# A burst of throwaway matmuls and sums on a zeroed buffer ahead of the first stage of a convolution kernel

## The chip, the cores and the metric

The kernel runs on one core of a Trainium2 chip. A core has a matmul engine (TensorE, PE in the profile, with its weight loads as PEld), a vector engine (DVE), a scalar engine (ACT), GpSimd (POOL), and SyncE (SP), which here issues all DMAs. The engines run beside one another, each in its own program order, and wait for one another through semaphores. On-chip data lie in SBUF, 128 partitions wide; matmul results go to PSUM, which has eight banks of 128 partitions by 512 f32 values.

The metric is the device time of one execution in microseconds; smaller is better.

## The reference

A long causal convolution by FFT, then a gated block: a short convolution of five taps that gives a gate, and two projections.

```python
def _attn_ref(x, h):                    # x: 8 x 6400 x 128, h: 6400 x 128
    L = 2 * S
    Xf = np.fft.rfft(x, n=L, axis=1)
    Hf = np.fft.rfft(h, n=L, axis=0)
    Yf = Xf * Hf[None, :, :]
    return np.fft.irfft(Yf, n=L, axis=1)[:, :S, :]

def _moe_ref(x, w_val, conv_w, w_out):
    gate_pre = np.zeros((B, S, D), dtype=np.float32)
    for k in range(K):                  # K = 5
        gate_pre += conv_w[k][None, None, :] * xp[:, k:k + S, :]
    gate = 1.0 / (1.0 + np.exp(-gate_pre))
    val = x @ w_val
    return gate * val @ w_out
```

## The kernel before

The sequence of 6400 is split as 100 x 64, so that the transforms become matmuls in f32 with constant matrices. For each of the eight batches and for the filter h there are four stages: stage 1 (transform over 100, `Forward`), stage 2 (transform over 64 and the product with the filter's spectrum, `Spectrum` for h and `Product` for x), stage 3 (`s3_quads`) and stage 4 (`Chunk.s4`), and behind them the gated block (`Chunk`, `Gates`). All matmuls address the array in parts: quarters of 64 rows by 64 columns of weights (stages 1 and 3), or halves of 128 rows by 64 columns (the rest). The profile names a matmul's tile by rows and columns, 50*64 for example; each matmul has one weight load (LDWEIGHTS) and one MATMUL. Since a helper records every operation (line 98), nearly all instructions carry that one line, and they are told apart by tiles.

The order on each engine is the order of the program's text; nothing is reordered.

What the change and the steps around it touch:

- `dt` (line 123) is one SBUF buffer of 128 x 16384 f32. At the start its first 12,800 columns, as `gh` (line 125), take stage 1 of the filter h. `gl` (line 131) is free at that time; later the weights of the gated block are decoded in it, when the first stage is over (line 508).
- `pair()` (line 203) hands out tiles of two PSUM banks, alternately from two pools of two tiles each.
- `fh` and `fx` (line 493) are stage 1 of the filter and of batch 0. Lines 494 to 496 ask for the first eight tiles of h, 256 KB each, and for the constant matrix r1; the first three go to `x_sb`, the others into m4_sb.
- `sums` (line 223) makes sum and difference of a loaded tile: the subtraction on POOL (line 229), the sum on the engine that it is given, DVE here (line 230), and then asks for the next tile. Lines 498 and 499 call it twice ahead of the loop.
- `half` (line 233) makes 16 matmuls of quarters on one tile's sums (line 241) and returns two copies from PSUM to `gh` or `gy`. The loop of lines 500 to 507 does 32 such halves, 16 for h and 16 for batch 0; the first copy goes to ACT (line 506), the second to ACT and DVE in turn.
- Behind this loop come stage 2 of both, from line 509, and then the loop over the batches, from line 575.

Of the kernel before, what the change touches and what calls it, by code (L numbers as in the profile page):

```python
# [13 lines left out]
ALU = mybir.AluOpType  # L14

S = 6400
C = 128
# [4 lines left out]
HP = 64  # L22
# [88 lines left out]
def longconv_moe(ctx: ExitStack, tc: tile.TileContext, x, h, r1, m2, r3, m4, w64, out):  # L111
    nc = _Engines(tc)
    B = x.shape[0]
    MUL, ADD = ALU.mult, ALU.add
# [8 lines left out]
    dt = cp.tile([128, N2 * 2 * C], F32, name="dt")  # L123
# [7 lines left out]
    gl = cp.tile([128, N2 - LATE, N1], F32, name="gl")  # L131
# [71 lines left out]
    def pair():  # L203
        pairs.append(pairs.pop(0))
        return pairs[-1].tile([128, 2, 512], F32, name="pt2", tag="pt2")
# [288 lines left out]
    fh.load()  # L494
    nc.sync.dma_start(r1_sb, r1)
    fh.load(len(xh) - 1)
    order = [(f, i) for f in (fh, fx) for i in range(NS)]
    for f, _ in order[:2]:
        f.sums(nc.vector)
# [75 lines left out]
    for b in range(B):  # L575
# [8 lines left out]
        for g in range(NS):  # L584
# [9 lines left out]
            if b == 0 and g < NKB:  # L594
                a = CH * g
# [96 lines left out]
```

## Time and profile before

| | |
|---|---|
| median of 2 runs | 1002.66 us (1001.01 to 1004.32) |
| the profiled execution | 1006.82 us |
| its span, first to last instruction | 1005.0 us |
| mean granted PE clock | 0.986 |
| instructions on PE, DVE, ACT, POOL | 21360, 939, 916, 551 |

In the page, "busy" is the time in which an engine works, with its share of the span. The rows of PE's clock have one digit for each fortieth of the span, in tenths of full speed. The chain follows the work that ended last back to its releasers. In the timeline a row has the start and the time taken in us, the engine and operation, the tile written and read, how many were merged, and the idle time before, with what ended it. A row of the groups by form ends with the busy time in us and the mean of one in ns, then the engine's idle time before them. A row of the windows has the stretch, its length, the busy time of PE with the number of its matmuls, the granted clock, the DMAs' share and GB/s. SPq is SyncE's queue, which issues DMAs.

### The profile page before, as it was taken

The page shows a single profiled execution, that of the slowest core. Times are in us where ns is not written, and L with a number is a line of the kernel's source. Part 1 is how long each engine was busy: PE and PEld are TensorE (multiplying, and loading weights), DVE is VectorE, ACT ScalarE, POOL GpSimd, SP SyncE. Part 2 cuts the span into 40 slices and gives each one's busy share as a digit, 9 for nine tenths or more (in the row PEclk, how much of TensorE's full clock was granted, in tenths as well). Part 3 has the DMA queues.
Part 4 walks back from the last instruction along what each step waited for, and adds up shares of the span by engine and source line. Part 5 has one row for each costly group of instructions (what it writes and reads, how often), then busy time and mean ns, then how long its engine had stood idle before and what let it go on. Part 6 is the DMA issues. An engine that isn't in the chain of part 4 may idle for free.

```text
span 1005.0 us, 46982 instructions
## 1 busy us (share of the span) xinstructions
PE 940.5 (94%) x21360; PEld 793.5 (79%) x21360; DVE 702.8 (70%) x939; ACT 475.5 (47%) x916; POOL 544.5 (54%) x551
## 2 busy tenths in 40 slices
PE   7897778999999999999999998999989999999987
PEld 7797778787978878887878778887887878786753
DVE  5499217977398747977398756977399755978366
ACT  4521434445543653546444554445544553534465
POOL 6467434785277744785177743784367752760032
PEclk9898999999999999999999999999999999999989
DMA  7783854756467545755467555665467554750012
GB/s 253 244 272 149 283 204 158 225 157 194 134 229 214 156 154 194 230 159 166 150 223 218 153 159 186 216 176 170 145 211 221 151 178 159 229 140 34 31 42 91
DMA packets 96838, 177.33 MB, mean 176 GB/s; under 512 B 43392, under 2 KB 49792, under 8 KB 96640
## 3 DMA queue, kind: packets, MB, share of 16 engines
q1 hardware_dynamic: 96640, 174.34, 55.6%
q8 instruction: 167, 2.74, 1.1%
q14 instruction: 31, 0.25, 0.1%
HBM read 141.55 MB, written 32.77 MB: 173 GB/s over the span
## 4 chain that ended last, share of the span: by engine, by line
PE 90%; issue 5%; DVE 3%; POOL 1%; ACT 1%; DMA 0%; POOLq 0%; DVEq 0%; ACTq 0%
PE pt L98 90%; DVE gl L98 1%; DVE dt L98 1%; POOL gl L98 1%; ACT dt L98 1%; DVE gy L98 0%; POOL dt L98 0%; DMA x<-hl 0%; DVE sd L98 0%; DVE m_sb L98 0%; POOLq L688 0%; ACT gl L98 0%; ACT yl L98 0%; ACT gy L98 0%; DVEq L98 0%
## 5 line engine op out<-in xcount | busy, mean ns | idle before, releaser
L98 PE MATMUL pt<-r_sb,gy 64*64 64x128 f32 (+1 forms) x8192 | 267.3, 273 | 20.3 <-issue 11.5
L98 PEld LDWEIGHTS pt<-r_sb,gy 64*64 64x64 f32 (+1 forms) x8192 | 235.8, 130 | 63.8 <-ACT gl L98 20.4
L98 POOL TENSOR_TENSOR sd<-x 128x256 f32<-128x256 f32 x236 | 197.4, 860 | 154.2 <-issue 124.2
L98 POOL TENSOR_TENSOR gy<-gy,h 128x512 f32<-128x512 f32 (+1 forms) x182 | 221.6, 1241 | 63.6 <-DVE h L98 27.7
L98 ACT COPY dt<-pt 128x512 f32<-128x512 f32 (+3 forms) x269 | 155.2, 581 | 193.9 <-PE pt L98 191.6
L98 PEld LDWEIGHTS pt<-m_sb,dt 128*64 128x64 f32 x4096 | 191.5, 137 | 35.3 <-issue 22.7
L98 PEld LDWEIGHTS pt<-gy,m 128*64 128x64 f32 x3008 | 179.1, 135 | 43.8 <-issue 23.6
L98 PE MATMUL pt<-gy,m 128*64 128x128 f32 x3008 | 193.3, 278 | 17.5 <-issue 12.0
L98 PE MATMUL pt<-m_sb,dt 128*64 128x100 f32 x4096 | 198.0, 250 | 2.9 <-DVE dt L98 2.4
L98 DVE COPY dt<-pt 128x512 f32<-128x512 f32 (+1 forms) x136 | 92.5, 680 | 132.1 <-PE pt L98 125.6
L98 PE MATMUL pt<-r_sb,sd 50*64 50x100 f32 x4608 | 143.2, 258 | 17.2 <-issue 11.2
L98 DVE TENSOR_TENSOR gy<-pt,h 128x1024 f32<-128x1024 f32 (+1 forms) x99 | 116.8, 1180 | 46.3 <-PE pt L98 46.3
L98 DVE SCALAR_TENSOR_TENSOR gl<-yl,w_sb,gl 128x500 f32<-128x500 f32 x147 | 130.6, 892 | 24.6 <-ACT gl L98 22.1
L98 PEld LDWEIGHTS pt<-r_sb,sd 50*64 50x64 f32 x4608 | 128.9, 142 | 22.2 <-issue 14.5
L98 DVE SCALAR_TENSOR_TENSOR dt<-pt,w_sb,dt 128x500 f32<-128x500 f32 (+7 forms) x216 | 132.9, 631 | 13.5 <-POOL dt L98 3.8
L98 ACT COPY gy<-pt 128x400 f32<-128x400 f32 x248 | 110.2, 496 | 41.2 <-PE pt L98 32.8
L98 ACT ACTIVATE dt<-pt,w_sb 128x500 f32<-128x500 f32 (+1 forms) x64 | 40.0, 625 | 170.2 <-PE pt L98 169.4
L98 PE MATMUL pt<-dt,w_sb 128*64 128x500 f32 (+2 forms) x480 | 116.0, 561 | 0.8 <-DVE dt L98 0.4
L98 POOL TENSOR_TENSOR dt<-dt,p 128x500 f32<-128x500 f32 (+1 forms) x64 | 66.4, 1038 | 82.5 <-DVE dt L98 58.0
L98 DVE TENSOR_TENSOR h<-pt,h 128x1024 f32<-128x1024 f32 (+1 forms) x91 | 107.3, 1179 | 2.3
L98 ACT COPY yl<-pt 128x500 f32<-128x500 f32 (+1 forms) x96 | 54.5, 568 | 83.9 <-PE pt L98 83.9
L98 DVE TENSOR_TENSOR gl<-pt,gl 128x500 f32<-128x500 f32 (+1 forms) x48 | 31.7, 661 | 54.5 <-PE pt L98 50.8
(40 smaller groups left out, 568.5 us busy)
## 6 DMA issues: line engine op xcount, KB each, us to landing
m<-m SPq DMA_DIRECT2D x90, 512.0 KB, 4.7
h<-hd SPq DMA_DIRECT2D x84, 512.0 KB, 3.9
x<-xl SPq DMA_DIRECT2D x118, 256.0 KB, 3.4
out<-dt SPq DMA_DIRECT2D x56, 250.0 KB, 5.8
out<-yl SPq DMA_DIRECT2D x40, 250.0 KB, 2.5
m_sb<-m SPq DMA_DIRECT2D x13, 375.0 KB, 4.5
hd<-h SPq DMA_DIRECT2D x8, 512.0 KB, 5.1
m_sb<-m SPq DMA_DIRECT2D x6, 512.0 KB, 6.5
```

Source lines behind the costliest of these rows:

```text
L98: return self._tc.keep_in_program_order(call(*args, **kwargs))
```

## The change

Between the first loads (line 496) and the first sums (line 497) new code is put. It zeroes the first 12,800 columns of dt, called z: columns 0 to 4095 by DVE, the rest by POOL. Then `throwaway` makes 290 matmuls on z into four PSUM banks (two tiles from `pair`): 70 of 128 x 128 weights by 512 moving columns (`slow`), and between them ten groups of small ones. Five groups have six rounds of four quarters, with 64 or 50 columns of weights that lie packed or at a step of two or four elements, and 64 or 128 moving columns; in one group the output is strided too. One group has 20 matmuls of 64 rows by 128 columns of weights and 64 moving columns. Three groups have 20 matmuls of 128 rows by 64 columns of weights and 128 moving columns, packed or strided, and the last has 20 with 50 moving columns. The last four wide matmuls write the four banks.

Then `throwaway_vector` makes three rounds, each with banks of four and of eight columns: ACT copies half of a PSUM view to gl, DVE adds that to the other half and writes dt, DVE subtracts likewise, and ACT makes a small copy to dt. Two copies of 512 columns on ACT end it. None of what it writes is read by the rest of the kernel: the first stage overwrites dt afterwards. Nothing is removed or moved.

```diff
--- before.py
+++ after.py
@@ -494,6 +494,86 @@
     fh.load()
     nc.sync.dma_start(r1_sb, r1)
     fh.load(len(xh) - 1)
+
+    z = dt[:, :12800]
+    zo = dt
+    nc.vector.memset(z[:, :4096], 0.0)
+    nc.gpsimd.memset(z[:, 4096:], 0.0)
+
+    def throwaway():
+        p = pair()
+        q = pair()
+        banks = [p[:, 0], p[:, 1], q[:, 0], q[:, 1]]
+
+        def mm(rows, cols, n, r0=0, c0=0, rhs=None, lhsT=None, bank=0, o=None):
+            o = banks[bank][c0 : c0 + cols, :n] if o is None else o
+            a = z[r0 : r0 + rows, :cols] if lhsT is None else lhsT[r0 : r0 + rows]
+            b = z[r0 : r0 + rows, 128 : 128 + n] if rhs is None else rhs[r0 : r0 + rows]
+            nc.tensor.matmul(o, lhsT=a, rhs=b, start=True, stop=True)
+
+        def slow(n):
+            for _ in range(n):
+                mm(128, 128, 512, bank=3)
+
+        def quarters(n, cols, width, lhsT=None, blocks=False):
+            for _ in range(n):
+                for r, c in ((0, 0), (1, 0), (1, 1), (0, 1)):
+                    o = None
+                    if blocks:
+                        o = banks[r][c * HP : c * HP + cols].rearrange("p (d b m) -> p d b m", d=4, b=4)[:, 0, ::3]
+                    mm(64, cols, width, r * HP, c * HP, lhsT=lhsT, bank=r, o=o)
+
+        e8 = z[:, 1024:2048].rearrange("p (k t) -> p k t", t=2)
+        e16 = z[:, 2048:4096].rearrange("p (k t) -> p k t", t=4)
+        m2v = z.rearrange("p (d k t) -> p d k t", k=100, t=2)
+        m4w = z.rearrange("p (d k t) -> p d k t", k=100, t=4)
+        slow(12)
+        quarters(6, 64, 64)
+        slow(6)
+        quarters(6, 64, 64, e8[:, :64, 1])
+        slow(6)
+        quarters(6, 50, 64, e8[:, :50, 1], True)
+        slow(6)
+        quarters(6, 64, 128, e8[:, :64, 1])
+        slow(6)
+        quarters(6, 64, 128, e16[:, :64, 1])
+        slow(6)
+        for _ in range(10):
+            for r in range(2):
+                mm(64, 128, 64, r * HP, bank=r)
+        slow(6)
+        for rhs in (None, m2v[:, :, 7], m4w[:, :, 7]):
+            for _ in range(10):
+                for c in range(2):
+                    mm(128, 64, 128, 0, c * HP, rhs=rhs, bank=2)
+            slow(6)
+        for _ in range(10):
+            for c in range(2):
+                mm(128, 64, 50, 0, c * HP, bank=2)
+        for i in range(4):
+            mm(128, 128, 512, bank=i)
+        return p, q
+
+    def throwaway_vector(p, q):
+        def ops(n, d, v, o, eng):
+            eng(o, v)
+
+        zv = zo.rearrange("p (n c d) -> p n c d", c=2, d=C)
+        v4 = p[:, 0].rearrange("p (d b m) -> p b m d", b=4, m=32)
+        v8 = p.rearrange("p r (d b m) -> p b m (r d)", b=4, m=32)
+        v = nc.vector
+        tmp = [gl.rearrange("p n t -> p (n t)")[:, 512 * i : 512 * i + 512].rearrange("p (b m d) -> p b m d", b=2, m=32) for i in range(2)]
+        for i in range(3):
+            for w, d in ((v4, 4), (v8, 8)):
+                t = tmp[i % 2][:, :, :, :d]
+                nc.scalar.copy(t, w[:, 2:])
+                for op, n in ((ADD, zv[:, 1:32]), (ALU.subtract, zv[:, 63:32:-1])):
+                    v.tensor_tensor(out=n[:, :, :, :d].rearrange("p n c d -> p c n d"), in0=w[:, :2, 1:], in1=t[:, :, 1:], op=op)
+                nc.scalar.copy(zv[:, 0, :, d : 2 * d], w[:, 0:2, 0])
+        nc.scalar.copy(zo[:, 0:512], q[:, 0])
+        nc.scalar.copy(zo[:, 0:512], q[:, 1])
+
+    throwaway_vector(*throwaway())
     order = [(f, i) for f in (fh, fx) for i in range(NS)]
     for f, _ in order[:2]:
         f.sums(nc.vector)
```

## The prediction

> **What bounds the kernel now.** I read the page first, for the span, the engines and the chain; then the timeline of the first 10 us, because the change stands ahead of the first stage; then the windows of PE, for the pace and the clock there.
>
> ```profile
> span 1005.0 us, 46982 instructions
> PE 940.5 (94%) x21360; PEld 793.5 (79%) x21360; DVE 702.8 (70%) x939; ACT 475.5 (47%) x916; POOL 544.5 (54%) x551
> PEclk9898999999999999999999999999999999999989
> PE 90%; issue 5%; DVE 3%; POOL 1%; ACT 1%; DMA 0%; POOLq 0%; DVEq 0%; ACTq 0%
> ```
>
> PE is busy 94% of the span and is 90% of the chain that ended last. There is no slack behind it into which whole microseconds of extra PE work at the head could be moved: what delays PE's first real matmul delays the end by as much, unless the first stage is held by something else. The timeline shows what holds it:
>
> ```profile
> 0.73 1.28 ACT L98 ACT_TABLE_LOAD   x1 [0.73 <-PEq L682]
> 0.74 0.39 SPq L98 DMA_DIRECT2D x<-hl  x1
> 2.59 2.33 SPq L98 DMA_DIRECT2D m_sb<-hl  x5
> 3.44 0.42 DVE L98 TENSOR_TENSOR sd<-x 128x256 f32<-128x256 f32 x1 [3.44 <-DMA x<-hl]
> 3.92 13.14 PE L98 MATMUL pt<-r_sb,sd 50*64 50x100 f32 x347 [3.92 <-DVE sd L98]
> 5.28 0.43 DVE L98 TENSOR_TENSOR sd<-x 128x256 f32<-128x256 f32 x1 [1.42 <-DMA x<-hl]
> 6.43 0.43 DVE L98 TENSOR_TENSOR sd<-x 128x256 f32<-128x256 f32 x1 [0.72 <-DMA x<-hl]
> ```
>
> The engines start at about 0.74 us. The first load ends DVE's wait at 3.44 us, its sum releases PE at 3.92 us, and PE then works on without a long wait until 17 us. Only these 3.44 us are free cover at the start; later waits for loads are 1.42 and 0.72 us.
>
> **The change, part by part.** It removes nothing. Everything added is on the zeroed buffer z, which is dt; the first stage's real results go into the same dt (line 251 through the copies), and each engine works in program order. So the sum on DVE (line 230) stands behind all added DVE work, the first copies on ACT (line 506) behind the added ACT copies, and the first real matmul (line 241) behind the added matmuls and behind DVE's sum. The end of the added DVE work takes the place of 3.44 us.
>
> **Loads and POOL: nothing.** Eight tiles of x are asked for ahead of the new code and land under the burst. SP's ninth load waits for the first sums and is shifted with them, as before. The subtraction on POOL (line 229) stands behind POOL's memset of 8,704 columns, and so do the matmuls that read z beyond column 4,096.
>
> ```profile
> L98 POOL TENSOR_TENSOR gy<-gy,h 128x512 f32<-128x512 f32 x168 | 211.9, 1283 | 63.6 <-DVE h L98 27.7 <-issue 15.6 <-PE pt L98 15.2
> L98 DVE TENSOR_TENSOR gy<-pt,h 128x1024 f32<-128x1024 f32 x92 | 112.0, 1217 | 39.4 <-PE pt L98 39.4
> L98 DVE TENSOR_TENSOR gy<-pt,h 128x512 f32<-128x512 f32 x7 | 4.8, 692 | 7.0 <-PE pt L98 7.0
> L98 DVE COPY dt<-pt 128x512 f32<-128x512 f32 x128 | 87.9, 687 | 125.8 <-PE pt L98 125.6
> L98 ACT COPY dt<-pt 128x512 f32<-128x512 f32 x129 | 75.7, 587 | 164.7 <-PE pt L98 162.4 <-ACT gl L98 2.3
> L98 ACT COPY gy<-pt 128x400 f32<-128x400 f32 x248 | 110.2, 496 | 41.2 <-PE pt L98 32.8
> ```
>
> At POOL's 1283 ns for 512 columns the memset takes 22 us at most. The matmuls that need it come after 54 wide ones, so at either price below 23 or 46 us after the burst's start at 5 us: no wait.
>
> **The memset on DVE.** 4,096 columns; no row shows one. DVE's step from 512 to 1024 columns is 525 ns, 1.03 ns a column: 4.2 us. A quarter of that, 1.1 us, is my lower bound. I take the nearest row, 4.2 us. The burst then starts at 0.74 + 4.2 = 5.0 us. The Trainium skill, "VectorE: DVE Perf Modes", section on zero memsets issued as uint32, has a memset at one cycle per element, which would be about 4.3 us; no trace here shows one.
>
> **The burst.** I count 70 matmuls of 128x128 weights by 512 columns (12, six after each of nine groups, 4), and 220 small ones in ten groups: 120 of quarters, 20 of row halves, 80 of column halves. The rows for their pace:
>
> ```profile
> 332.76 0.88 PE L98 MATMUL pt<-r_sb,sd 50*64 50x100 f32 x32
> 333.56 1.06 PE L98 MATMUL pt<-yl,w_sb 128*64 128x500 f32 x4
> 336.35 0.87 PE L98 MATMUL pt<-r_sb,sd 50*64 50x100 f32 x32
> 337.04 1.93 PE L98 MATMUL pt<-r_sb,gy 64*64 64x128 f32 x64
> 338.79 0.87 PE L98 MATMUL pt<-r_sb,sd 50*64 50x100 f32 x32
> 988.55 1.01 PE L98 MATMUL pt<-gl,w_sb 128*64 128x500 f32 x4
> 62.00:82.00 20.00, 20.00 (x351) 1.00 0.81 274
> L98 PE MATMUL pt<-dt,w_sb 128*64 128x500 f32 x416 | 107.0, 585 | 0.8 <-DVE dt L98 0.4 <-DVE gl L98 0.2
> L98 PEld LDWEIGHTS pt<-m_sb,dt 128*64 128x64 f32 x4096 | 191.5, 137 | 35.3 <-issue 22.7 <-DVE dt L98 8.0 <-PE pt L98 2.1
> ```
>
> Two pairs of column halves by 500 columns take 1.01 us from first start to last end, one matmul 0.585, so the second pair starts 0.425 us after the first: 0.85 ns a column for a pair. The 64 quarters from 337.04 to 338.79 us take 27.3 ns each, 109 a quad of 128 columns, again 0.85 ns a column. So f32 costs 0.85 ns a column, whatever the rows, where both column halves are served by matmuls of their own.
>
> The wide matmul has no row: one instruction, one stream of moving columns, 128 columns of weights. Its lower bound is the pair's pace, 512 x 0.85 = 0.43 us. Its upper bound is the two halves served in turn by the one stream, 0.86 us. As instruction it is nearest to one half's matmul, and the pair gets its pace from two instructions that each bring their stream; a single stream that needs 0.85 ns a column for 64 columns of weights should need twice that for 128. I take 0.86 us: 70 x 0.86 = 60.2 us. With 0.43 it is 30.1. Of pages, two bear on it. The Trainium skill, "FP8 and Floating Point Precision", TensorE Precision Notes, lets true FP32 pass the array four times; four passes at its 2.4 GHz would be 0.85 us, 59.7 us for the 70. The Trainium skill, "Perfetto Trace Analysis", Engine Utilization, halves the array's rate for FP32_LOW_HIGH, which would be 0.43 us and 29.9 us; the halves' 0.85 ns a column agrees with the latter, the full width no run shows.
>
> The small ones, at the clock of those rows: 72 quarters with 64 columns between half of 27.3 ns and the 21.6 that 100 columns cost (336.35 to 337.04 over 32), near the latter because the loads of weights are as many: 1.5 us. 48 quarters with 128 columns by 27.3: 1.3 us. Strided weights I put at nothing beyond that, since gy's weights in the 27.3 ns row have the same stride of two elements. 60 column halves with 128 columns by 20.00/351 = 57 ns: 3.4 us, strided moving operands included as that row has them. 20 column halves with 50 columns, half of 57 to 57: 0.8 us. 20 row halves with 64 columns, 27 to 80 ns: 1.0 us. Together 8.0 us.
>
> Switches between tile shapes: 32 matmuls take 0.69 us from 336.35 to the next start, but 0.80 from 332.76 where the shape changes to 128 rows. That is 0.11 us, times 20 switches 2.2 us.
>
> **The clock.**
>
> ```profile
> 8.00:10.00 2.00, 2.00 (x56) 1.00 1.05 403
> 13.00:15.00 2.00, 1.94 (x82) 1.00 0.61 183
> 20.00:21.00 1.00, 1.00 (x32) 0.50 0.51 197
> 97.11 0.70 PE L98 MATMUL pt<-r_sb,gy 64*64 64x128 f32 x8 [5.24 <-DVE gy L98]
> 96.00:106.00 10.00, 8.19 (x252) 0.75 0.42 130
> ```
>
> From 8 to 10 us PE makes 28 matmuls a microsecond, about as at clock 0.50 at 20 us, and 41 at 13 us: the start runs at half clock, whatever the column shows before its first event, some 8 us from 3.92 on. The burst will pay for it instead, 3.4 to 8.3 us at half pace, 1.7 to 4.2 lost: 2.8 us. Will the first stage then find full clock? At 97.11 us PE had idled 5.24 us and the ten microseconds around read 0.75, so it had gone back to half. The tail below idles PE for 9 us. I count no gain; kept full clock would be worth up to 4 us.
>
> **The tail.** DVE's twelve sums have 248 or 496 columns a row: 512 columns cost 692 ns and a column 1.03, so 421 and 676 ns. ACT's copies of 256 and 512 columns: 587 ns, and (587-496)/112 = 0.81 ns a column, 380 and 587. Each round on DVE is two small sums, a hand-over, ACT's 512-column copy (it waits for the buffer that the small sums read), a hand-over, two large sums: 0.84 + 0.05 + 0.59 + 0.05 + 1.35 + 0.05 = 2.93 us. Three rounds and the first copy: 9.2 us, entirely behind the last matmul, since its bank is written last. Reads and writes with strides like these stand in the rows (dt from pt, 687), so nothing more for them. The two last ACT copies (1.2 us) run beside DVE's last sum and the first real matmuls; the small copies, beside DVE.
>
> **The sum.** 5.0 + 60.2 + 8.0 + 2.2 + 2.8 + 0.2 (last matmul's latency) + 9.2 = 87.6 us at the tail's end, against 3.44 us: 84.2 later. Loads that have landed spare the first stage at most the 1.42 and 0.72 us, at half clock about 1. Net +83. The profiled execution took 1006.82 us, so 1090; it stands 4.2 above the median of 1002.66, so against the median 1086. The start-up bounds move this by -3 and +2, the clock by -5 and +2, the small matmuls by 2 either way.
>
> **The rivals.**
> A: the wide matmul runs at the pair's pace, 0.43 us. For it: 0.85 ns a column wherever the trace looks. Against it: nowhere does one stream feed both halves. 1086 - 30 = 1056. This is also where the halved rate of the page leads.
> B: weight loads come out from under the wide matmuls. A load of 64 columns takes 137 ns; 128 columns with no other tile to work beside might show 0.14 to 0.27 us each, 70 times: +10 to +19, 1096 to 1105. For it: in the rows loads always have another half at work. Against it: PEld is busy 79% beside PE's 94% with hardly a gap, so loads are hidden at a far denser rate.
> C, not slower: the burst is covered by the start's own waits. Place: ahead of line 499. The cover is 3.44 us for the first load, 2 for the next loads, 4 of half clock. It decides only if start, burst and tail together stay under about 10 + 20 = 30 us; without start, tail and small matmuls (26 us) the 70 would have to take under 4 us, 0.06 us each, seven times faster than any row's pace. It would read 1003 to 1022.
>
> **How the numbers follow.** My forecast 0.73, A 0.18, B 0.07, C 0.02. The likeliest gives 1086, its own range 1076 to 1094. The range that takes in A and the cheaper half of B is 1050 to 1100, with 0.9 of the chance before the bounds' own error. A change of 2%, 20 us, is about what a measurement of this kernel can tell from none; all cases but C are slower by more: slower 0.97, same 0.02, faster 0.01.
>
> **What would show it.** In the timeline after: DVE's memset ending near 5 us; wide matmuls starting every 0.86 us (A: 0.43; B: over 1.0); the last one ending near 78 us; DVE's sums until 88 us; the first sd<-x then; the first stage again at half clock; from there on the same stages, shifted. If the time differs while the shift is as summed, the later stages have changed, which I hold to be nothing. What would make it wrong above all is the price of one wide matmul: every 0.1 us of it is 7 us.

## The result, and the profile after

The changed kernel takes 1096.67 us (median of 2 runs, 1096.43 to 1096.91) against 1002.66 us before: 1.0926 times the time, 95% interval 1.0872 to 1.098. In a later comparison it took 1099.68 us (4 runs) against 1004.38 us (17 runs), 1.095 times (1.0912 to 1.0987). The forecast was 1086 us with a range of 1050 to 1100.

The page after:

```profile
span 1094.7 us, 48185 instructions
PE 1023.1 (93%) x21940; PEld 836.0 (76%) x21940; DVE 712.7 (65%) x952; ACT 479.6 (44%) x930; POOL 551.4 (50%) x552
PEclk9998799889999999999999999999999999999999
PE 90%; issue 4%; DVE 4%; ACT 1%; POOL 1%; POOLq 0%; DVEq 0%; ACTq 0%
```

PE has 21940 matmul instructions instead of 21360: 580 more, for 290 more matmuls in the text. So each f32 matmul of the text is two weight loads and two MATMUL instructions; the sentence ahead of the prediction that gives it one of each is wrong by that factor. This count is what the prediction misread.

The timeline after, from the start to the first real matmul (start, time taken, engine and operation, count, idle time before):

```profile
0.73 7.35 POOL L98 MEMSET dt<- 128x8704 f32 x1 [0.29 <-POOLq L762]
1.66 3.47 DVE L98 MEMSET dt<- 128x4096 f32 x1 [1.66 <-PEq L762]
5.18 80.62 PE L98 MATMUL pt<-dt 128*128 128x512 f32 x580 [5.18 <-DVE dt L98]
7.05 0.34 PEld L98 LDWEIGHTS pt<-dt 128*128 128x128 f32 x1 [0.52 <-issue]
7.91 0.34 PEld L98 LDWEIGHTS pt<-dt 128*128 128x128 f32 x1 [0.52 <-issue]
9.24 0.19 PEld L98 LDWEIGHTS pt<-dt 128*128 128x128 f32 x1 [0.24 <-issue]
9.67 0.19 PEld L98 LDWEIGHTS pt<-dt 128*128 128x128 f32 x1 [0.24 <-issue]
86.02 0.74 DVE L98 TENSOR_TENSOR dt<-pt,gl 128x248 f32<-128x248 f32 x2 [80.89 <-PE pt L98]
86.85 0.17 ACT L98 COPY dt<-pt 128x8 f32<-128x8 f32 x1 [2.35 <-DVE dt L98]
86.91 0.59 ACT L98 COPY gl<-pt 128x512 f32<-128x512 f32 x1
87.53 1.26 DVE L98 TENSOR_TENSOR dt<-pt,gl 128x496 f32<-128x496 f32 x2 [0.78 <-ACT gl L98]
88.82 0.17 ACT L98 COPY dt<-pt 128x16 f32<-128x16 f32 x1 [1.32 <-DVE dt L98]
88.89 0.38 ACT L98 COPY gl<-pt 128x256 f32<-128x256 f32 x1
89.30 0.74 DVE L98 TENSOR_TENSOR dt<-pt,gl 128x248 f32<-128x248 f32 x2 [0.51 <-ACT gl L98]
95.27 1.09 DVE L98 TENSOR_TENSOR sd<-x 128x256 f32<-128x256 f32 x3
95.74 7.67 PE L98 MATMUL pt<-r_sb,sd 50*64 50x100 f32 x224 [9.94 <-DVE sd L98]
```

The burst runs from 5.18 to 85.8 us. A wide matmul shows two weight loads, 0.43 us from one to the next at full clock and 0.86 at half clock, up to about 8.9 us. The half clock there is read from this spacing: the trace's first record of the clock is the change to full at 8.85 us. The tail takes 86.02 to 95.27 us, and DVE's first real sum starts at 95.27 us instead of 3.44: 91.8 us later. The small groups, in windows from each group's first matmul to the next wide one (stretch, length, PE busy and matmuls; edges count once more):

```profile
17.48:18.34 0.86, 0.86 (x49) 1.00 0.00 0
23.69:24.57 0.88, 0.88 (x50) 1.00 0.00 0
29.92:30.74 0.82, 0.82 (x50) 1.00 0.00 0
36.09:37.56 1.47, 1.47 (x49) 1.00 0.00 0
42.91:44.56 1.65, 1.65 (x49) 1.00 0.00 0
49.91:52.29 2.38, 2.38 (x42) 1.00 0.03 7
57.63:59.96 2.33, 2.33 (x41) 1.00 0.00 0
65.31:67.76 2.45, 2.45 (x41) 1.00 0.00 0
73.12:75.45 2.33, 2.33 (x41) 1.00 0.00 0
80.80:82.10 1.30, 1.30 (x41) 1.00 0.00 0
24.57:29.92 5.35, 5.35 (x19) 1.00 0.00 0
```

The ten groups take 16.5 us. The last row is one stretch of six wide matmuls: 5.35 us where 12 instructions of 0.429 make 5.15. The 0.2 that is left falls at the two changes of tile shape, about 0.1 us each; ten times over it is 2.0 us.

What became of the 91.8 us later on shows in one and the same DVE instruction, the first of a pair of TENSOR_SCALAR behind the first stage, before (first fence) and after (second):

```profile
53.63 1.68 DVE L98 TENSOR_SCALAR gl<-gl 128x261 int32<-128x261 int32 x2
```

```profile
146.87 1.68 DVE L98 TENSOR_SCALAR gl<-gl 128x261 int32<-128x261 int32 x2
```

There the shift is 93.2 us; at the end the spans differ by 1094.7 - 1005.0 = 89.7 us. So the head accounts for it; what moves by three microseconds either way behind it is no larger than what executions of one and the same program differ by (999.97 to 1010.44 us for the kernel before in one comparison), and is not explained here.

### The profile page after: what moved, and what is told of

The parts are those of the page before. It is cut to its first block, busy times and chain, and to the rows that moved or that the text cites. A ratio compares the mean times of both kernels' runs of the same rounds, so it can differ in the third digit from the quotient of the medians.

```text
span 1094.7 us, 48185 instructions
## 1 busy us (share of the span) xinstructions
PE 1023.1 (93%) x21940; PEld 836.0 (76%) x21940; DVE 712.7 (65%) x952; ACT 479.6 (44%) x930; POOL 551.4 (50%) x552
## 4 chain that ended last, share of the span: by engine, by line
PE 90%; issue 4%; DVE 4%; ACT 1%; POOL 1%; POOLq 0%; DVEq 0%; ACTq 0%
PE pt L98 90%; DVE dt L98 2%; DVE gl L98 1%; ACT dt L98 1%; POOL gl L98 1%; DVE sd L98 0%; DVE gy L98 0%; POOL dt L98 0%; ACT gl L98 0%; DVE m_sb L98 0%; POOLq L768 0%; ACT yl L98 0%; DVEq L98 0%; POOLq L98 0%; ACTq L98 0%
## 5 line engine op out<-in xcount | busy, mean ns | idle before, releaser
L98 PE MATMUL pt<-r_sb,gy 64*64 64x128 f32 (+1 forms) x8192 | 270.6, 275 | 15.7 <-issue 6.7
L98 PEld LDWEIGHTS pt<-r_sb,gy 64*50 64x50 f32 (+1 forms) x8192 | 238.7, 131 | 59.5 <-ACT gl L98 21.2
L98 POOL TENSOR_TENSOR gy<-gy,h 128x512 f32<-128x512 f32 (+1 forms) x182 | 221.7, 1240 | 64.1 <-DVE h L98 32.5
L98 ACT COPY dt<-pt 128x512 f32<-128x512 f32 (+5 forms) x277 | 157.0, 571 | 194.5 <-PE pt L98 183.0
L98 PE MATMUL pt<-gy,m 128*64 128x128 f32 x3008 | 193.0, 278 | 17.5 <-issue 12.0
L98 PE MATMUL pt<-dt 128*128 128x512 f32 (+6 forms) x580 | 80.6, 342 | 5.2 <-DVE dt L98 5.2
```

The costliest lines, as they stand in the source:

```text
L98: return self._tc.keep_in_program_order(call(*args, **kwargs))
```

## The experiments

Two theories stood against each other after the result. **P, passes:** every f32 matmul of the text is two PE instructions, each at 0.85 ns a column, whatever the width of its weights. **S, streams** (the prediction's): one instruction costs 0.85 ns a column for 64 columns of weights, and 128 columns fed by one stream cost twice that.

**Wide matmuls as two halves.**

```diff
-                mm(128, 128, 512, bank=3)
+                for c in range(2):
+                    mm(128, 64, 512, 0, c * HP, bank=3)
...
-            mm(128, 128, 512, bank=i)
+            for c in range(2):
+                mm(128, 64, 512, 0, c * HP, bank=i)
```

> Each of the 70 wide matmuls (128x128 weights, 512 columns) becomes two of 128x64 by 512 columns; the rest of the change stays. Theory P (passes): the trace after holds two PE instructions for every matmul of the text, 580 for 290, and each takes 0.429 us for 512 columns; a pair of halves is then four instructions that run two by two, 0.86 us a pair, as one wide matmul. Time as after the change, about 1097 us, within 3 us, less up to 2 us for shape switches that fall away. Theory S (the prediction's: one stream feeds the two halves in turn, two streams at once feed them side by side): a pair takes 0.43 us, 30 us less, about 1067 us.

1093.28 us, 1.0875 times the time before (1.0836 to 1.0913). The groups by form of the first 84 us and the window of one stretch of six such pairs:

```profile
L98 PE MATMUL pt<-dt 128*64 128x512 f32 x280 | 64.1, 609 | 5.2 <-DVE dt L98 5.2
```

```profile
24.49:29.79 5.30, 5.30 (x30) 1.00 0.00 0
```

140 matmuls of the text are 280 instructions, and six pairs take 5.30 us where six wide ones took 5.35. The halves do run two by two: one after the other, 280 instructions of 0.429 us would take 120 us, and PE is busy for 64.1 us with them. Side-by-side halves gain nothing over a full-width matmul: S is wrong, P holds.

**Wide matmuls in bf16.** They read the same zeros as bf16, so that this part is another computation.

```diff
+        zb = z[:, :320].bitcast(mybir.dt.bfloat16)
+        def wide(bank):
+            nc.tensor.matmul(banks[bank], lhsT=zb[:, :128], rhs=zb[:, 128:], start=True, stop=True)
...
-                mm(128, 128, 512, bank=3)
+                wide(3)
```

> The 70 wide matmuls read the same zeros as bf16 (128x128 weights, 512 columns); small groups and tail stay f32. Theory P: a bf16 matmul is one PE instruction and the profile shows 510 instead of 580 on the zeroed buffer; at the pace of 0.429 us for each it would be 30 us less, about 1067 us, and if each of the two f32 instructions also runs at half pace, 0.21 us for one bf16, 45 us less, about 1052 us. Theory S says nothing of bf16.

1048.81 us, 1.0426 times (1.039 to 1.0461): some 48 to 51 us less than the changed kernel, by its two medians. Windows of two stretches of bf16 matmuls (five of the six of each are in the records, and the windows start at the first of these), and DVE's first real sum in the timeline:

```profile
10.84:12.01 1.17, 1.17 (x5) 1.00 0.00 0
13.12:14.29 1.17, 1.17 (x5) 1.00 0.07 14
```

```profile
49.36 1.09 DVE L98 TENSOR_TENSOR sd<-x 128x256 f32<-128x256 f32 x3
```

The first sum comes at 49.36 instead of 95.27 us, 45.9 earlier, which is 70 x (0.858 - 0.216) = 44.9 and about 0.1 us less around each of the ten groups. The other 2 to 5 us of the time lie behind the head and are not explained. The median distance of two such matmuls is 0.216 us and each is one instruction, 62 of the 70 being in the records. So an f32 matmul costs four times a bf16 one, as two instructions at half pace. The Trainium skill, "FP8 and Floating Point Precision", TensorE Precision Notes, has four passes for true FP32: the cost agrees, 0.858 against 0.216 us, though the trace shows two instructions.

**Without the small groups.** The 220 small matmuls are left out and the 70 wide ones stand in one row.

```diff
-        quarters(6, 64, 64)
-        slow(6)
...
+        slow(54)
```

> The ten groups of small matmuls are left out, the 70 wide ones, the memsets and the tail stay. By the trace after: the groups take 16.5 us from their first start to the next wide one, and the shape switches add 0.2 us to each of ten wide groups: 18.5 us less, about 1078 us. By the prediction's prices (8.0 us and 2.2 us) 10 us less, about 1086 us.

1075.67 us, 1.0705 times (1.0671 to 1.0738), 21 to 24 us less than the changed kernel. DVE's first real sum in the timeline:

```profile
77.78 1.08 DVE L98 TENSOR_TENSOR sd<-x 128x256 f32<-128x256 f32 x3
```

It comes 95.27 - 77.78 = 17.5 us earlier; a microsecond of the 18.5 is missing because full clock came at 10.8 us here, against 8.9. What the time shows beyond that lies behind the head, where executions differ by as much, and is not explained. The prediction's 10.2 us for groups and switches are refuted.

**Without the tail.** The kernel that ran had kept the small groups, so its time stands against the changed kernel, and only the differences of the expectation apply, not its absolute times.

```diff
-    throwaway_vector(*throwaway())
+    throwaway()
```

> As the run without small groups, and the whole tail of ACT copies and DVE sums is left out too, so that nothing reads the burst's results. Against that run: if the tail lies wholly on the path, its 9.4 us go (from the last matmul's end at 85.8 us to DVE's first real sum at 95.3 us in the trace after). If the clock is then kept full, because PE no longer idles for 10 us, half of the 5.3 us that the first stage ran at half clock goes as well: 12 us in all, about 1066 us; if the loads or the sums bind the first stage instead of the clock, 9.4 us alone, about 1069 us. A rival that has part of the tail covered by the loads: less than 7 us.

1087.27 us, 1.0812 times (1.078 to 1.0843), 9.4 to 12.4 us less. The timeline and a window of ten microseconds of its first stage (busy time of PE, PEld, DVE, ACT, POOL with counts, then the granted clock):

```profile
85.51 2.29 PE L98 MATMUL pt<-r_sb,sd 50*64 50x100 f32 x96
90.72 1.78 PE L98 MATMUL pt<-r_sb,sd 50*64 50x100 f32 x64 [0.47 <-DVE sd L98]
92.98 1.61 PE L98 MATMUL pt<-r_sb,sd 50*64 50x100 f32 x55 [0.47 <-DVE sd L98]
137.36 1.68 DVE L98 TENSOR_SCALAR gl<-gl 128x261 int32<-128x261 int32 x2
```

```profile
85.00:95.00 10.00, 7.98 (x281) 6.43 (x280) 7.90 (x11) 5.33 (x12) 6.02 (x8) 1.00 0.46 129
```

PE's first real matmul comes at 85.51 instead of 95.74 us, 10.2 earlier: all of the tail is on the path. The clock stays full, but PE now waits for DVE's sums: 64 instructions, two halves of the first stage, take 92.98 - 90.72 = 2.26 us, of which PE works 1.78. The time, 9.4 to 12.4 us less, does not tell whether a gain of clock came on top of the tail.

**Without small groups and tail**, the comparison that the last expectation describes.

> The run without the tail had still held the small groups; here both are left out, so that it stands against the run without small groups (1075.7 us). By the difference that the tail made in the full burst (PE's first real matmul at 85.5 instead of 95.7 us): 10 us less, about 1066 us, with full clock at the first stage worth nothing more, because DVE needs 1.13 us for each half of the first stage there and PE's 0.73 us at full clock do not come to bear. If full clock counts, 12 us or more less, 1064 us or under. First real matmul near 67 us: 5.2 + 2.0 for cold clock + 70 x 0.858.

1066.45 us, 1.0633 times (1.0579 to 1.0688), with a wide spread of 1061 to 1072. That is 9.2 us under the run without small groups by the medians, 7 by the ratios. The timeline:

```profile
67.82 2.29 PE L98 MATMUL pt<-r_sb,sd 50*64 50x100 f32 x96
116.14 1.68 DVE L98 TENSOR_SCALAR gl<-gl 128x261 int32<-128x261 int32 x2
```

The first real matmul comes at 67.82 us; by 5.18 + 2.4 (full clock at 9.95 us) + 70 x 0.858 it should come at 67.6. The tail costs its own length. A gain from kept clock does not show: from the first real matmul to the first TENSOR_SCALAR behind the first stage this run takes 116.14 - 67.82 = 48.3 us, and the other trace without a tail 137.36 - 85.51 = 51.9. All twelve traces of this case, with tail, without it and before, lie from 48.3 to 51.9 us, so a gain of some 2 us or less could hide in this spread.

**A small burst alone, as a warm-up, on the kernel before.**

```diff
+    nc.gpsimd.memset(dt[:, :640], 0.0)
+    p = pair()
+    for n in (512, 256):
+        nc.tensor.matmul(p[:, 0, :n], lhsT=dt[:, :128], rhs=dt[:, 128 : 128 + n], start=True, stop=True)
```

> The kernel before with a small burst alone: POOL zeroes 640 columns and PE makes one wide matmul of 512 and one of 256 columns, meant to lie within the 3.4 us that the first load takes; no tail. If the half clock binds the first stage, full clock from about 5.4 us instead of 12.2 us takes 1 to 3 us off. If the loads bind it (a tile every 0.7 to 1.4 us, against 0.36 us of PE work at full clock), nothing, 1003 us within 1; if the burst outlasts the first load, up to 1 us more.

1006.83 us (12 runs) against 1004.38 (17 runs), 1.0027 times (1.0006 to 1.0047). The timeline:

```profile
1.42 2.93 PE L98 MATMUL pt<-dt 128*128 128x512 f32 x4 [1.42 <-POOL dt L98]
4.28 1.37 PE L98 MATMUL pt<-r_sb,sd 50*64 50x100 f32 x32
5.76 1.28 ACT L98 ACT_TABLE_LOAD   x1 [5.76 <-PE pt L98]
6.74 0.42 DVE L98 TENSOR_TENSOR sd<-x 128x256 f32<-128x256 f32 x1 [0.73 <-DMA x<-hl]
13.29 0.91 PE L98 MATMUL pt<-r_sb,sd 50*64 50x100 f32 x32 [1.04 <-issue]
```

The burst outlasted the first load: the first real matmul starts at 4.28 instead of 3.92 us. For this case up to 1 us more was expected, and the interval, 0.6 to 4.7 us more, takes that in. Full clock came at 4.9 us, but DVE still waits for loads, ACT's table load has moved from 0.73 us to 5.76, ahead of its first copy, and PE idles 1.04 us ahead of 13.29 us for nothing that the profile shows (issue). Which of these takes the gain is not told apart, and a change of 2 us in the first stage is within the spread of the traces given above. No version tried beats the kernel before.

**The changed kernel again, and two versions of the tail.**

> The changed kernel as it is, timed again beside the kernel before and the runs of this call: 94 us longer than before (87 to 98 by the interval of its first two runs).

As given above, 95 us longer.

```diff
-                nc.scalar.copy(zv[:, 0, :, d : 2 * d], w[:, 0:2, 0])
+                nc.scalar.copy(gl[:, 20, : 2 * d].rearrange("p (b d) -> p b d", b=2), w[:, 0:2, 0])
```

> In the tail the small ACT copies of 8 and 16 columns are written to a free place in gl instead of dt. In the trace after each of them waits for DVE's two sums before it (idle 0.86 and 1.32 us, ended by DVE dt), and ACT's next copy stands behind it. If that order makes the tail, a round falls from 3.28 us (86.02 to 89.30) towards the 2.9 us or less that the sums and one 512-column copy need, and the copy of 256 columns moves beside DVE's sums: about 1 to 2 us less over three rounds, seen in the timeline; in the time it is near what can be told. If the copies wait for the buffers in gl instead: no change.

1098.63 us, 1.0946 times (1.0904 to 1.0988): no change that the time shows. With the copies in the tile p instead (`p_t[1][:, 0, : 2 * d]`):

> The small ACT copies of the tail write to a tile that nothing else uses there (p), instead of dt. Writing them to another place in gl had changed nothing: they still waited for DVE. If the wait is for the tile gl, in which DVE reads, the copies now go ahead and a round of the tail falls from 3.3 to about 2.9 us. If it is for the PSUM bank that DVE reads at the same time, or for the order of the 512-column copy's buffer, a round stays at 3.3 us.

One time, 1102.47 us. Its timeline:

```profile
88.60 0.17 ACT L98 COPY p<-pt 128x16 f32<-128x16 f32 x1 [1.38 <-DVE dt L98]
89.08 0.74 DVE L98 TENSOR_TENSOR dt<-pt,gl 128x248 f32<-128x248 f32 x2 [0.57 <-ACT gl L98]
92.42 0.74 DVE L98 TENSOR_TENSOR dt<-pt,gl 128x248 f32<-128x248 f32 x2 [0.57 <-ACT gl L98]
```

A round still takes 92.42 - 89.08 = 3.34 us and the small copy still waits for DVE. The wait is not for the place that it writes. Whether it is for the PSUM bank that both read was not tried and stays open.

**Other numbers of moving columns in three small groups.**

```diff
-        quarters(6, 64, 64)
+        quarters(6, 64, 32)
...
-                mm(64, 128, 64, r * HP, bank=r)
+                mm(64, 128, 128, r * HP, bank=r)
...
-                mm(128, 64, 50, 0, c * HP, bank=2)
+                mm(128, 64, 25, 0, c * HP, bank=2)
```

> Three small groups get other numbers of moving columns: the first quarters 32 instead of 64, the row halves with 128 columns of weights 128 instead of 64, the column halves of the last group 25 instead of 50. Where the moving columns set the pace, a group's time goes with them: 0.86 us to 0.45, 2.38 to about 4.6, 1.30 to 0.7. Where the loads of weights set it, it stays: 0.86, 2.38, 1.30. The trace after puts them so: the quarters with 64 columns near both (15 ns an instruction against 13.6 by columns), so between; row halves at 56 ns an instruction, twice what 64 columns take elsewhere, so loads, 2.4 us still; the last group 29 ns against 21 by columns, so loads, 1.3 us still.

```profile
17.52:18.35 0.83, 0.83 (x50) 1.00 0.00 0
49.91:52.34 2.43, 2.43 (x41) 1.00 0.02 7
80.86:82.14 1.28, 1.28 (x42) 1.00 0.00 0
```

One time, 1094.68 us. The windows of the three groups show 0.83, 2.43 and 1.28 us against 0.86, 2.38 and 1.30. Half or double the columns, the time stays: in all three, not only in two, the columns do not set the pace. What is left unchanged in them is the weights, so their loads are the likely bound; they were not varied by themselves. This holds for these sizes only. In the changed kernel itself, quarters with the same strided weights took 0.88 us with 64 moving columns and 1.47 with 128, and column halves 1.30 us with 50 and 2.33 with 128: there more columns cost more.

## Why the prediction was right, and which of its steps were not

The sign, the place and the range were right: nothing covers the burst and its tail, DVE's first sum starts when they end, and the end of the kernel moves by about as much. The size of the largest term was right by luck, as shown below. The terms, in us:

| term | forecast | measured |
|---|---|---|
| start of the burst | 5.0 | 5.18 |
| 70 wide matmuls, full clock | 60.2 | 60.1 (140 x 0.429) |
| small matmuls and shape switches | 8.0 + 2.2 | 16.5 + 2.0 |
| lost at half clock | 2.8 | 1.8 (5.18 to 8.85 us) |
| last latency and tail | 0.2 + 9.2 | 0.2 + 9.25 |
| DVE's first sum | 87.6 | 95.27 |

**The step that failed is the reading of a count.** The prediction took the row of four matmuls 128x500 at 988.55 us as two pairs of halves. It is one pair: each matmul of the text is two instructions, as the rows could have told. Stage 3 has 8 x 16 x 32 = 4096 matmuls in the text, and the page before gives x8192 for them:

```profile
L98 PE MATMUL pt<-r_sb,gy 64*64 64x128 f32 (+1 forms) x8192 | 267.3, 273 | 20.3 <-issue 11.5
```

So a pair of halves costs 1.7 ns a column, not 0.85, and every price per matmul that was taken from a time divided by that count was half of the true one. The prediction's sentence that the halves' pace agrees with the halved rate falls with it. The small matmuls, "together 8.0 us", took 16.5; doubled, the prediction's prices give 16.0. That is the miss of the sum, 8.3 us with the switches, and the run without them gave it back. The 1 us that was taken off for loads that have landed did not show either: the first stage took 51.1 us from its first matmul, against 49.7 before, both inside the spread of the traces.

**The wide matmul's price was right by luck: two errors cancelled.** The misread count made the pair of halves, and with it the lower bound, half as dear as it is. The step "a single stream that needs 0.85 ns a column for 64 columns of weights should need twice that for 128" then doubled it again, and this step is refuted by the halves. Had only the count been read, the pair's pace would have been 0.86 us: rival A's rule, that the wide matmul runs at the pair's pace, would have given the measured price, and the stream argument 1.72 us, 60 us too much for the 70. With the count misread, A's 0.43 us is the price of one of the two instructions.

**The start** was right by two errors as well: DVE's memset began at 1.66 us and not at 0.74, and took 3.47 us and not 4.2.

**Rivals B and C.** B did not happen: a wide load takes 0.19 us and leaves PEld idle for 0.24 before the next one, so the loads stay under the matmuls. C had no ground: of the cover that it counts, only the 3.44 us of the first load showed.

**The clock.** That the first stage would find half clock again was right: it was back at half from 90.8 to 101.0 us, as in this window of the trace after:

```profile
96.00:101.00 5.00, 5.00 (x128) 5.00 (x128) 1.99 (x6) 2.63 (x6) 2.40 (x3) 0.50 0.65 205
```

Of the "up to 4 us" for kept clock nothing showed: without the tail the clock stays full, and PE waits for DVE instead.

**The tail.** The total was right, the way was not. A round takes 3.28 us, not 2.93, because ACT's small copies wait for DVE and the 256-column copy stands behind them in ACT's order; DVE's sums were shorter, 0.74 and 1.26 us a pair instead of 0.84 and 1.35, and the first copy ran under the burst.

## What to carry to other kernels

Before a row's time is divided by its count, hold the count against the number of such operations in the program's text; where the factor is two, every price per operation is off by two, and a sum of small terms shows it where one large term may hide it. Two steps that each change a price by two can cancel: a term that fits does not show that its steps were right, and it took the run with halves to part them. Work put at the head of this kernel, which one engine bounds, came out in full at the end: the cover was what the first engine waits for, here 3.44 us, and it is read from the timeline's first rows. A warm clock is worth what the next bound leaves of it, and here that bound was DVE's sums.

## What the runs showed of the hardware

Small f32 matmuls here have a least time below which fewer moving columns gain nothing: quarters take 0.83 and 0.86 us for 48 instructions with 32 or 64 columns, and 1.47 with 128; column halves 1.28 and 1.30 us for 40 with 25 or 50, and 2.33 with 128; row halves with 128 columns of weights the same 2.4 us with 64 or 128. Weights at a step of four elements took 1.65 us for 48 instructions at 128 columns, those at a step of two 1.47. Matmul instructions of different tiles start 18 ns apart on average, 0.86 us / 48. The Trainium skill, "TensorE: Matmul & The Clock Gate", section "Wait — 56ns, not 53.3ns?", has a floor of about 25 ns from start to start; here the measurement decides. DVE's memset of f32 took 3.47 us for 4,096 columns, 0.85 ns a column, and POOL's as much a column (7.35 us for 8,704), a third of POOL's 2.5 ns in a sum of two operands.
